# Attention with a forget gate and a SwiGLU block on one Trainium2 core: gate rows sent straight to their places, narrower crossbar turns, a clip on another engine, more fillers and a new order

## The chip, the cores and the metric

The kernel runs on one core of a Trainium2 chip. The core has five engines with instruction queues of their own: TensorE (PE in the profile; its weight loads are the row PEld), VectorE (DVE), ScalarE (ACT), GpSimd (POOL) and SyncE (SP, which here only issues DMAs). Each runs its own instructions in order and waits on semaphores for the others. TensorE writes to PSUM, which has eight banks of 128 x 512 fp32; ACT and DVE read from there. The metric is the device time of one execution in microseconds; each kernel has several runs, and their median counts.

## The reference

```python
scores = scale * np.matmul(q, k.transpose(0, 1, 3, 2))
log_f = np.log(np.clip(f, 0.0001, 1.0))
cum = np.cumsum(log_f, axis=-1)
decay = cum[:, :, :, None] - cum[:, :, None, :]
causal = np.triu(np.ones((S, S), dtype=bool), k=1)
scores = np.where(causal, -1000000000.0, scores + decay)
scores = scores - np.max(scores, axis=-1, keepdims=True)
attn = np.exp(scores)
attn = attn / (np.sum(attn, axis=-1, keepdims=True) + 1e-09)
return np.matmul(attn, v).astype(np.float32)
```

That is the attention, with 8 batches, 8 heads, 576 positions and 64 channels a head; scale is 1/8. Its output, laid out as x with 4608 tokens of 512 channels, goes through the feed-forward part with a width of 1536:

```python
g = x @ w_gate
silu = g * (1.0 / (1.0 + np.exp(-g)))
val = x @ w_val
return (silu * val @ w_out).astype(np.float32)
```

Inputs and output are fp32; inside, the kernel multiplies in bf16.

## The kernel before, in words

**Attention.** A head's scores are computed transposed, keys on the partitions. The causal half is cut into blocks of 128 keys by up to 320 queries, grouped into four PSUM banks (`BANKS`). For each bank PE computes the scores (`score`, L650; `score2`, L668 to L680, for batch 0), ACT takes the exponential into bf16 (`expo`, L684, tiles PTa for bank 0 and PT for the others), POOL zeroes the triangle above the diagonal (`mask`, L693), and PE multiplies the result with the values and a column of ones (`weigh`, L707). DVE divides by the sum (L714, L719), and PE transposes the head pair (`flip`, L724) and ACT or DVE copies it to xT (`put`), or a crossbar DMA does both (`cross`, L735).

**The decay.** The decay is added by the same matmul: beside the 64 channels, queries and keys have four more rows (partitions 64 to 67 of QK). On the query side they hold 8 times the cumulated logarithm and three rows of ones, on the key side one row of ones and the cumulated logarithm, times -8, in three bf16 parts. `gates` makes them: loads of f on SP and ACT, a clip (L334), the logarithm on ACT (L337), the scan on DVE (L341), then `hi`, `less`, `mid`, `less`, `low` (L346 to L357), in two column halves of 256 and 320 for the 16 heads of batches 0 and 1. Batch 0 reads its rows in place. For batch 1, `dec_out` writes four rows per head to a DRAM tensor, `blank` writes the ones there, and `rows` (L549) brings all of them to QK, a DMA per head pair. The other 48 heads (`lf1`, `cum1`) have a clip of their own on POOL, a logarithm on ACT, and their scan and parts later on. ACT loads the table of the Exp function (L478, `o_warm`) after all of these logarithms.

**Queries and keys.** Batch 0 and 1: POOL issues DMAs that convert to bf16 (`ld_quad`, L501), PE transposes (`turn_two`, L509, and `turn`, L525), and ACT or DVE copies from PSUM to QK, putting the columns in order (`straighten`, through L310 for ACT and L312 for DVE and POOL). Batches 2 to 7: a DMA on POOL's queue narrows a pair of heads to bf16 in DRAM (`narrow`), and two crossbar transposes on SP (`turned`, L546), one each for queries and keys, bring it to QK. A turn writes all 128 partitions, so `rows` follows it and overwrites partitions 64 to 67.

**The feed-forward part.** For each tile of 512 tokens: gate and value matmuls (L852; four accumulating matmuls are one group), the tanh on ACT (L856), two products on DVE (L860, L863), the projection (L867), a copy on ACT (L871), and the store on SP (L874). The first four chunks of the first tile are done in two halves of 256 tokens. Weights come by DMAs on POOL's queue (L845, L848).

**What sets the order.** Nothing is ordered by hand in the program text. Every step is an `Op` with the engines that can do it, an estimated duration, what it comes after, the buffers that it takes, a key and perhaps an earliest time. `Plan.run` walks through time, and whenever an engine is free it starts, of the steps that are ready and whose buffers are free, the one with the lowest key; that sequence becomes the engine's program order. A copy that ACT or DVE can do goes to whichever takes it first. The table `ORDER` replaces the key of a step by its number, counted in the order of creation. Where PE has nothing to start before 22 us of planned time (`IDLE_TO`), a filler matmul (`dummy`, L954) of 256 columns is put in, into a free bank of the pool f. Batches from 2 on are released at planned times, `PACE0` for the first of them.

Of the kernel before, what the change touches and what calls it, by code (L numbers as in the profile page):

```python
# [10 lines left out]
BF16 = mybir.dt.bfloat16  # L11
# [23 lines left out]
class Plan:  # L35
# [32 lines left out]
    def run(self, idle=None):  # L68
# [30 lines left out]
        while left:  # L99
# [45 lines left out]
            for e in engines:  # L145
                while busy[e] <= t + 1e-9:
# [61 lines left out]
PACE0 = 59.0  # L208
# [4 lines left out]
def kernel(ctx, tc, q, k, v, f, w_gate, w_val, w_out, out):  # L213
    nc = tc.nc
# [24 lines left out]
    qk_dram = nc.dram_tensor("qk_d", (2 * B, HSD + D), BF16, kind="Internal").ap()  # L239
# [116 lines left out]
    def low(e, c):  # L356
        nc.vector.tensor_scalar(out=KG[:, c], in0=r1[:, c], scalar1=ct[:, 2:3], scalar2=ct[:, 3:4], op0=ALU.mult, op1=ALU.add)  # L357
# [11 lines left out]
    def dec_out(e, b, n):  # L369
        g = slice(H, 2 * H) if b else slice(2 * H, BH)  # L370
        src = KG[2 * H * ((n - 1) % 4) + H :][:H] if b else late[n][2 * H :]
        nc.sync.dma_start(out=dec_dram[0, 0, g] if n == 0 else dec_dram[n, 1, g], in_=src)
# [13 lines left out]
    def gates(parts, key):  # L386
# [10 lines left out]
        for i, c in enumerate(parts):  # L397
# [3 lines left out]
            a = op(("DVE", 0.05 + w * 0.0011), hi, c, after=[s], key=kk, tag="hi")  # L401
            a = op(("DVE", 0.1 + w * 0.00155), less, 0, c, after=[a, o_ct], key=kk)
            a = op(("DVE", 0.05 + w * 0.0011), mid, c, after=[a], key=kk)
            a = op(("DVE", 0.1 + w * 0.00155), less, 1, c, after=[a], key=kk)
            a = op(("DVE", 0.05 + w * 0.0011), low, c, after=[a], key=kk, tag="low")
# [5 lines left out]
        outs = [op(("SP", SPi), dec_out, 1, n, after=ends, key=-7, dma=0.1, packet=50, tag="decout") for n in range(4)]  # L411
# [7 lines left out]
        out1 = [op(("SP", SPi), dec_out, 0, n, after=l, key=9000, ready=DECOUT_AT, dma=0.25, packet=50, tag="decout") for n in range(4)]  # L419
# [4 lines left out]
    def blank(e, what):  # L424
# [6 lines left out]
        elif what == "edge":  # L431
            nc.sync.dma_start(out=qk_dram[:, HSD:], in_=QK[: 2 * B, 0, 1, 2 * S :])
        elif what == "ones":
            E[e].memset(ones.bitcast(F32), ONE2)
        elif isinstance(what, tuple) and what[0] == "ones_q":
            nc.sync.dma_start(out=dec_dram[0, 1, what[1]], in_=ones[what[1]])
        elif isinstance(what, tuple):
            n = what[1].stop - what[1].start
            nc.sync.dma_start(out=dec_dram[1:, 0, what[1]].rearrange("r h s -> h r s"),
                              in_=ones[what[1]].unsqueeze(1).to_broadcast([n, 3, S]))  # L440
# [25 lines left out]
        else:  # L466
# [16 lines left out]
    o_edge = op(("SP", SPi), blank, "edge", after=[o_qkz], key=900, dma=0.2, ready=22)  # L483
    o_out1, o_out2 = [[op(("SP", SPi), blank, (x, c), after=[o_ones], key=1, dma=0.06 * n, packet=50, ready=t) for x in ("ones_q", "ones_k")]
                      for c, n, t in ((slice(0, 2 * H), 1, 4), (slice(2 * H, BH), 6, ONES_AT))]
# [56 lines left out]
    def turned(e, p, x):  # L542
        b, r = divmod(p, FB)
        lo = (2 * b + x) * (HSD + D) + 2 * r * S * D
        src = bass.AP(qk_dram.tensor, qk_dram.offset + lo, [[D, 2 * S], [1, P]])
        nc.sync.dma_start_transpose(out=QK[:, hqk[p].i, x, : 2 * S], in_=src)  # L546
# [23 lines left out]
    def values(b, n, key, ready=0.0):  # L570
# [9 lines left out]
        o = op(("SP", 0.9), ld_v, b, n, bv, after=held, behind=rows1 if b == 1 else out1 if b == 2 else [], take=[] if held else [bv], use=[bv] if held else [], key=key, dma=0.6 if last else 1.2, ready=ready, tag=("v", b, n))  # L580
# [10 lines left out]
    turns, rows1 = [], []  # L591
# [14 lines left out]
    def quad(b, g, key, ready=0.0):  # L606
# [12 lines left out]
        for u in range(2):  # L619
# [3 lines left out]
            for j in range(2):  # L623
                q_ready[2 * p + j] = done[u] + [r]
# [452 lines left out]
```

## Time and profile before

| | us |
|---|---|
| median of 3 runs | 383.69 (383.54 to 383.76) |
| the profiled execution | 383.79 |
| its span, first to last instruction | 382.0 |
| PE busy in the span | 373.3 |
| DVE, ACT, POOL busy | 217.6, 212.6, 142.9 |
| granted TensorE clock | 1.000 of full |

Each row of a stretch table gives the stretch, its length, then for each engine the busy time and in brackets the number of instructions. Rows of a timeline give start, duration, engine, line, operation, output and input tiles with their shapes, and in square brackets the idle time of the engine before it and what ended that. Adjacent instructions of one kind are merged to one row with their count. A matmul's duration includes its passage through the array, so that the durations of pipelined matmuls overlap. Rows of the chain of waits give start, time and work. Lines are those of the kernel before.

### The profile page before, as it was taken

The page shows a single profiled execution, that of the slowest core. Times are in us where ns is not written, and L with a number is a line of the kernel's source. Part 1 is how long each engine was busy: PE and PEld are TensorE (multiplying, and loading weights), DVE is VectorE, ACT ScalarE, POOL GpSimd, SP SyncE. Part 2 cuts the span into 40 slices and gives each one's busy share as a digit, 9 for nine tenths or more (in the row PEclk, how much of TensorE's full clock was granted, in tenths as well). Part 3 has the DMA queues.
Part 4 walks back from the last instruction along what each step waited for, and adds up shares of the span by engine and source line. Part 5 has one row for each costly group of instructions (what it writes and reads, how often), then busy time and mean ns, then how long its engine had stood idle before and what let it go on. Part 6 is the DMA issues. An engine that isn't in the chain of part 4 may idle for free.

```text
span 382.0 us, 8349 instructions
## 1 busy us (share of the span) xinstructions
PE 373.3 (98%) x3129; PEld 207.5 (54%) x3129; DVE 217.6 (57%) x454; ACT 212.6 (56%) x435; POOL 142.9 (37%) x369
## 2 busy tenths in 40 slices
PE   5999999999999999999999999999999999999996
PEld 4677665455555555555655555555654444444444
DVE  8887976277516771377326761576327815733750
ACT  4999872266466565844766466557763323323322
POOL 8996656035443453535463346513430000000000
PEclk9999999999999999999999999999999999999999
DMA  8999998759979975999799959993431011002003
GB/s 144 181 192 189 210 227 144 192 96 173 194 179 192 182 155 132 208 177 190 153 216 220 172 94 247 191 181 63 69 89 45 2 55 55 2 27 83 3 0 110
DMA packets 125000, 51.88 MB, mean 136 GB/s; under 512 B 111840, under 2 KB 119360, under 8 KB 124192
## 3 DMA queue, kind: packets, MB, share of 16 engines
q1 hardware_dynamic: 108608, 36.14, 47.2%
q0 software_dynamic: 16288, 15.14, 26.4%
q8 instruction: 24, 0.39, 0.4%
q14 instruction: 16, 0.13, 0.1%
q10 hardware_dynamic: 64, 0.07, 0.1%
HBM read 38.56 MB, written 17.07 MB: 146 GB/s over the span
## 4 chain that ended last, share of the span: by engine, by line
PE 93%; ACT 5%; issue 1%; DVE 1%; POOL 0%; ACTq 0%; POOLq 0%
PE ps L852 49%; PE ps L867 24%; PE ps L650 10%; PE ps L707 7%; ACT PT L684 1%; ACT QK L310 1%; PE ps L954 1%; ACT PTa L684 1%; PE ps L724 1%; ACT L478 0%; POOL xT L501 0%; PE ps L668 0%; ACT xT L310 0%; DVE xn L719 0%; PE ps L676 0%
## 5 line engine op out<-in xcount | busy, mean ns | idle before, releaser
L852 PE MATMUL ps<-xT,wv 128*128 128x512 bf16 (+1 forms) x448 | 111.5, 371 | 0.0
L856 ACT ACTIVATE th<-ps 128x512 f32<-128x512 f32 (+1 forms) x112 | 65.2, 583 | 83.0 <-PE ps L852 81.8
L852 PE MATMUL ps<-xT,wg 128*128 128x512 bf16 (+1 forms) x448 | 111.4, 371 | 0.0
L860 DVE SCALAR_TENSOR_TENSOR th<-th,ps 128x512 f32<-128x512 f32 (+1 forms) x112 | 74.5, 666 | 62.3 <-ACT th L856 61.9
L867 PE MATMUL ps<-wo,hh 128*128 128x512 bf16 (+2 forms) x456 | 104.9, 368 | 0.0
L684 ACT ACTIVATE PT<-ps 128x512 bf16<-128x512 f32 (+2 forms) x192 | 91.6, 513 | 15.5 <-PE ps L650 10.8
L863 DVE TENSOR_TENSOR hh<-th,ps 128x512 bf16<-128x512 f32 (+1 forms) x112 | 74.7, 668 | 13.0 <-PE ps L852 2.8
L693 POOL TENSOR_SCALAR_AFFINE_SELECT PT<-PT 128x128 bf16<-128x128 bf16 (+1 forms) x192 | 53.2, 283 | 54.1 <-ACT PT L684 48.7
L650 PE MATMUL ps<-QK 68*128 68x256 bf16 (+2 forms) x392 | 63.7, 260 | 0.8 <-ACT QK L310 0.6
L852 PEld LDWEIGHTS <-wg 128*128 128x128 bf16 x448 | 42.5, 97 | 40.4
L852 PEld LDWEIGHTS <-wv 128*128 128x128 bf16 x448 | 42.2, 97 | 39.7
L867 PEld LDWEIGHTS <-hh 128*128 128x128 bf16 x456 | 41.5, 97 | 36.3 <-issue 0.3
L693 POOL TENSOR_SCALAR_AFFINE_SELECT PTa<-PTa 128x256 bf16<-128x256 bf16 x64 | 26.1, 416 | 86.2 <-ACT PTa L684 84.7
L714 DVE RECIPROCAL rc<-ps 128x5 f32<-128x5 f32 (+2 forms) x68 | 12.9, 190 | 68.9 <-PE ps L707 68.2
L871 ACT ACTIVATE ot<-ps 128x512 f32<-128x512 f32 (+2 forms) x38 | 21.9, 575 | 52.2 <-PE ps L867 48.6
L707 PE MATMUL ps<-VB,PT 128*128 128x65 bf16 x768 | 43.7, 193 | 0.0
L707 PEld LDWEIGHTS <-PT 128*128 128x128 bf16 x768 | 35.7, 97 | 13.4 <-POOL PT L693 1.2
L650 PEld LDWEIGHTS <-QK 68*128 68x128 bf16 x392 | 31.9, 97 | 19.0 <-issue 1.4
L684 ACT ACTIVATE PTa<-ps 128x384 bf16<-128x384 f32 x64 | 30.9, 487 | 10.8 <-PE ps L650 10.8
L719 DVE TENSOR_TENSOR xn<-ps,rc 128x320 bf16<-128x320 f32 (+2 forms) x72 | 32.3, 454 | 2.3
L312 POOL CAST VB<-natv 128x512 bf16<-128x512 f32 (+1 forms) x32 | 19.0, 616 | 0.4 <-DMA natv<-in_v_dram 0.4
L707 PEld LDWEIGHTS <-PTa 128*128 128x128 bf16 x192 | 13.1, 97 | 10.9 <-POOL PTa L693 0.6
(71 smaller groups left out, 158.7 us busy)
## 6 DMA issues: line engine op xcount, KB each, us to landing
out_dram<-ot SPq DMA_DIRECT2D x35, 256.0 KB
natv<-in_v_dram SPq DMA_DIRECT2D x25, 256.0 KB
qk_d<-in_q_dram POOLq DMA_DIRECT2D x24, 144.0 KB, 3.6
qk_d<-in_k_dram POOLq DMA_DIRECT2D x24, 144.0 KB, 4.4
wv<-in_moe_w_val_dram POOLq DMA_DIRECT2D x3, 512.0 KB, 12.8
wg<-in_moe_w_gate_dram POOLq DMA_DIRECT2D x3, 512.0 KB, 10.1
wo<-in_moe_w_out_dram POOLq DMA_DIRECT2D x4, 384.0 KB, 15.6
xT<-in_q_dram POOLq DMA_DIRECT2D x4, 288.0 KB, 7.4
```

Source lines behind the costliest of these rows:

```text
L312: E[e].tensor_copy(dst, src)
L650: nc.tensor.matmul(s[:, c : c + w], QK[:KR, hqk[p].i, 1, j * S + kt * P : j * S + (kt + 1) * P], QK[:KR, hqk[p].i, 0, j * S + q0 : j * S + ...
L684: nc.scalar.activation(place(h, i)[:, OFFS[i] : OFFS[i] + c], ps(bs)[:, :c], AF.Exp, scale=0.125)
L693: nc.gpsimd.affine_select(out=d, in_=d, pattern=pat, compare_op=ALU.is_ge, fill=0.0, base=0, channel_multiplier=-1,)
L707: nc.tensor.matmul(o[:, lo : lo + D + 1], pt[:, c : c + P], VB[hvb[b].i][:, kt, hb, : D + 1], start=first and n == 0, stop=last and n == l ...
L719: nc.vector.tensor_mul(XN[bx.i][:, qb : qb + nq, j], o, r)
L852: nc.tensor.matmul(ps(bf)[:, :n], w[:, ko, fc * P : (fc + 1) * P], xT[:, ko, t0 : t0 + n], start=(ko == 0), stop=(ko == KD - 1))
L856: nc.scalar.activation(TH[bt.i][:, :n], ps(bf)[:, :n], AF.Tanh, scale=0.5)
L860: nc.vector.scalar_tensor_tensor(out=t, in0=t, scalar=1.0, in1=ps(bf)[:, :n], op0=ALU.add, op1=ALU.mult)
L863: nc.vector.tensor_mul(HH[bh.i][:, lo : lo + n], TH[bt.i][:, :n], ps(bf)[:, :n])
L867: nc.tensor.matmul(ps(bf)[:m, c], HH[hs[fc].i][:, lo : lo + m], wo[:, fc, c], start=(fc == 0), stop=(fc == KF - 1))
L871: nc.scalar.activation(OT[bo.i][:m, c], ps(bf)[:m, c], AF.Copy, scale=0.5)
```

## The change

1. Batch one's gate rows: eight copies `dec_in`, each of one row of four heads, go from the tile of the gates straight to QK, and four copies fill the rows of ones there. The two writes of ones to DRAM cover the other heads alone, and batch 1 has no `rows`.
2. `turned` reads 64 columns instead of 128 and writes partitions 0 to 63 alone. So `rows` touches nothing that a turn writes; it takes the slot and is issued ahead of the turns. The pad at the end of the DRAM tensor and the DMA that filled it go.
3. The clip of the 48 other heads is done by DVE instead of POOL.
4. `low` is a scalar_tensor_tensor whose second tensor is a broadcast column, instead of a tensor_scalar with two columns.
5. Fillers go to any free bank of the pools o, f and t, in that order, instead of f alone.
6. Some estimates of the planner (among them `TWARM`, the time from which it takes matmuls at full speed, and the cost of turns, straightens, `hi` and `mid`), `PACE0`, and the table `ORDER` are new. The exponentials of bank 0 of batch 0 name the Exp table's load as a predecessor. Steps of batch 0's second part and of the feed-forward part have a number higher by one than before.

```diff
-                        if e == "PE" and idle and idle[0].done is not None and idle[0].done <= t < idle[1] and self.free["f"]:
-                            idle[2](self.free["f"][-1])
+                        spare = [(p, self.free[p][-1]) for p in ("o", "f", "t") if self.free[p]]
+                        if e == "PE" and idle and idle[0].done is not None and idle[0].done <= t < idle[1] and spare:
+                            idle[2](spare[0])
...
-PACE0 = 59.0
+PACE0 = 58.0
...
     def low(e, c):
-        nc.vector.tensor_scalar(out=KG[:, c], in0=r1[:, c], scalar1=ct[:, 2:3], scalar2=ct[:, 3:4], op0=ALU.mult, op1=ALU.add)
+        nc.vector.scalar_tensor_tensor(out=KG[:, c], in0=r1[:, c], scalar=ct[:, 2:3], in1=ct[:, 3:4].to_broadcast([P, c.stop - c.start]),
+                                       op0=ALU.mult, op1=ALU.add)
...
-    def dec_out(e, b, n):
-        g = slice(H, 2 * H) if b else slice(2 * H, BH)
-        src = KG[2 * H * ((n - 1) % 4) + H :][:H] if b else late[n][2 * H :]
-        nc.sync.dma_start(out=dec_dram[0, 0, g] if n == 0 else dec_dram[n, 1, g], in_=src)
+    def dec_out(e, n):
+        g = slice(2 * H, BH)
+        nc.sync.dma_start(out=dec_dram[0, 0, g] if n == 0 else dec_dram[n, 1, g], in_=late[n][2 * H :])
+
+    def dec_in(e, n, j):
+
+        lo = 2 * H * ((n - 1) % 4) + H + j
+        dst = QK[D + n : D + n + 1, 2 : 2 + FB, min(n, 1), j * S : (j + 1) * S]
+        nc.sync.dma_start(out=dst, in_=KG[lo : lo + H - 1 : 2])
...
-        outs = [op(("SP", SPi), dec_out, 1, n, after=ends, key=-7, dma=0.1, packet=50, tag="decout") for n in range(4)]
+        outs = [op(("SP", SPi), dec_in, n, j, after=ends, key=-7 + 0.1 * j, dma=0.05, packet=50, tag="decin") for j in range(2) for n in range(4)]
...
+            w, j = what
+            r = slice(D, D + 1) if w else slice(D + 1, KR)
+            dst = QK[r, 2 : 2 + FB, w, j * S : (j + 1) * S]
+            nc.sync.dma_start(out=dst, in_=ones[: r.stop - r.start].unsqueeze(1).to_broadcast([r.stop - r.start, FB, S]))
...
-        lo = (2 * b + x) * (HSD + D) + 2 * r * S * D
-        src = bass.AP(qk_dram.tensor, qk_dram.offset + lo, [[D, 2 * S], [1, P]])
-        nc.sync.dma_start_transpose(out=QK[:, hqk[p].i, x, : 2 * S], in_=src)
+        lo = (2 * b + x) * HSD + 2 * r * S * D
+        src = bass.AP(qk_dram.tensor, qk_dram.offset + lo, [[D, 2 * S], [1, D]])
+        nc.sync.dma_start_transpose(out=QK[:D, hqk[p].i, x, : 2 * S], in_=src)
...
-            r = op(("SP", SPi), rows, p, after=[o_qkz] + out0 + o_out1, use=[hqk[p]], key=key, dma=0.25, ready=ready, tag=("rows", p))
-            rows1.append(r)
             for j in range(2):
-                q_ready[2 * p + j] = done[u] + [r]
+                q_ready[2 * p + j] = done[u] + out0[4 * j : 4 * j + 4] + o_out1[2 * j : 2 * j + 2]
...
-        ts = []
+        done = [op(("SP", SPi), rows, p, after=out1 + o_out2, take=[hqk[p]], use=[hqk[p]], key=key - 1, dma=0.25,
+                   ready=release(p) - ROWS_LEAD, tag=("rows", p))]
         for x in range(2):
-            ts.append(op(("SP", 1.45), turned, p, x, after=[narrowed[x], o_edge] + out1, behind=ts, take=[] if x else [hqk[p]],
-                         use=[hqk[p]] if x else [], key=key, dma=1.6, ready=release(p), tag=("turned", p)))
-        done = ts + [op(("SP", SPi), rows, p, after=ts + out0 + out1 + o_out2, use=[hqk[p]], key=key + 3, dma=0.25,
-                        tag=("rows", p))]
+            done.append(op(("SP", TURN_SP), turned, p, x, after=[narrowed[x]] + out1, behind=done, use=[hqk[p]] if x else [],
+                           key=key, dma=TURN_DMA, ready=release(p), tag=("turned", p)))
...
-TWARM = 8.3
+TWARM = 7.5
...
-CLIP1 = ("POOL", 2.2)
+CLIP1 = ("DVE", 0.75)
```

Of the new table, some entries, by step number. On DVE: `hi` of the first half 18 (-233.2), `less` 19 (-333.1), `mid` 20 (-73.1347), `less` 21 and `low` 22 (-115.6), the second scan 24 (197.6), the clip of the other heads 42 (-73.1347), the pad clears 59 (379.0), the ones 60 (59.8). Before, the pad clears had -78.4, the ones -14.0, and the clip -15.0. On ACT: the logarithm of the other heads 43 (-283.5) and the table's load 54 (-283.5), before -13 and -143.4. The straightens of the second pair of head pairs of batch 0, 80, 82, 84 and 86, have -87.8, -98.4, -13.7 and 59.8. On PE: the gate groups 1536 (1302.9) and 1516 (1570.7), before 100200 and 100000; the score groups 273 (1535.7) and 280 (1565.1) of batch 0's last heads; its last flips 289 and 293 (2012.1 and 1985.6).

More of the change, by code (lines that the diff above doesn't have):

```diff
@@ L418, in gates @@
             l.append(a)
-        out1 = [op(("SP", SPi), dec_out, 0, n, after=l, key=9000, ready=DECOUT_AT, dma=0.25, packet=50, tag="decout") for n in range(4)]
+        out1 = [op(("SP", SPi), dec_out, n, after=l, key=9000, ready=DECOUT_AT, dma=0.25, packet=50, tag="decout") for n in range(4)]
         return done, lns + [l1], outs, out1
@@ L589, in values @@
                 o.after.append(v_ready[b, 0])
-    turns, rows1 = [], []
+    turns = []
     def four(g, key):
```

36 lines of the change are left out of this document (17 added, 19 removed), and 92 rows, old and new, of the table ORDER.

## The prediction

> **What bounds the kernel now.** I began with the page's table of engines, and then took the busy time by stretch, cut where the chain of waits changes its character.
>
> ```profile
> PE 373.3 (98%) x3129; PEld 207.5 (54%) x3129; DVE 217.6 (57%) x454; ACT 212.6 (56%) x435; POOL 142.9 (37%) x369
> ```
> ```profile
> 0.00:7.20 7.20, 3.60 (x18) 2.32 (x20) 5.58 (x35) 2.79 (x5) 6.00 (x13) 1.00 0.74 125
> 7.20:16.00 8.80, 7.88 (x211) 5.88 (x213) 8.44 (x32) 8.11 (x16) 8.66 (x12) 1.00 1.56 177
> 16.00:24.00 8.00, 7.76 (x131) 5.21 (x127) 5.70 (x21) 8.00 (x22) 7.99 (x21) 1.00 1.39 202
> 24.00:31.65 7.65, 7.02 (x164) 5.59 (x159) 6.52 (x19) 7.28 (x16) 7.49 (x21) 1.00 1.55 186
> 31.65:60.00 28.35, 28.33 (x255) 18.56 (x253) 22.99 (x47) 23.50 (x53) 16.67 (x42) 1.00 1.18 204
> 60.00:368.50 308.50, 308.30 (x2293) 164.01 (x2292) 167.20 (x303) 160.16 (x321) 96.05 (x265) 1.00 0.67 128
> 368.50:382.00 13.50, 10.39 (x72) 5.92 (x70) 1.15 (x2) 2.73 (x6) 0.00 (x0) 1.00 0.22 78
> ```
>
> The columns are the length, then PE, PEld, DVE, ACT and POOL (busy us and instructions), the granted clock, the DMA share and GB/s. From 31.65, where the first gate matmul of the feed-forward part begins, to 368.5, PE is busy 336.63 of 336.85 us. Nothing that a DMA, VectorE or GpSimd does there can shorten the run unless PE gets less work, and the change removes no useful matmul. The last 13.5 us are the last projections and stores, which the diff leaves alone. So the change is decided in the first 31.65 us, and there ACT (23.39 of 24.45 us from 7.20 on) and POOL (24.14) are full, while PE stands still 24.45 - 22.66 = 1.79 us and fills part of the rest with filler matmuls. The chain of waits says which of the two full engines it is:
>
> ```profile
> 3.60 3.59 PE ps L954 x16
> 7.86 2.28 ACT QK L310 x4
> 10.14 0.54 ACT QK L337
> 10.70 1.28 ACT L478
> 13.46 0.53 ACT QK L310
> 17.80 2.89 ACT PT L684 x7
> 29.01 0.74 ACT QK L310
> 30.05 0.54 PE ps L650 x4
> 31.81 0.44 PE ps L852 x4
> ```
>
> Columns: start, length, work. Fillers (L954) hold PE until the first turned queries, then from 7.86 to about 20.7 (17.80 + 2.89) the chain is nearly ACT alone: straightens (L310), the logarithm of the other heads (L337), the load of the Exp table (L478), exponentials (L684). Later it alternates between PE, VectorE and ACT until the gates begin. The reader should see that a microsecond comes off the run only if ACT's chain shrinks or starts sooner, or if PE is given gate matmuls to do while it waits for ACT.
>
> **The change part by part.** The rows that price it:
>
> ```profile
> 7.54 2.14 POOL L334 TENSOR_SCALAR QK<-QK 64x576 f32<-64x576 f32 x1
> 3.74 1.42 DVE L334 TENSOR_SCALAR xT<-xT 64x256 f32<-64x256 f32 x4
> 6.96 0.48 DVE L350 SCALAR_TENSOR_TENSOR xT<-xT,ct 128x256 f32<-128x256 bf16 x1
> 7.48 0.88 DVE L357 TENSOR_SCALAR xT<-xT,ct 128x256 bf16<-128x256 f32 x1
> 11.01 0.65 DVE L430 MEMSET PT<- 128x32 f32 x15
> 11.58 0.71 DVE L312 COPY QK<-ps 128x576 bf16<-128x576 bf16 x1
> 12.30 0.30 DVE L434 MEMSET ot<- 64x288 f32 x1
> 13.67 0.62 DVE L350 SCALAR_TENSOR_TENSOR xT<-xT,ct 128x320 f32<-128x320 bf16 x1
> 14.32 0.92 DVE L357 TENSOR_SCALAR xT<-xT,ct 128x320 bf16<-128x320 f32 x1
> 15.27 1.66 SPq L372 DMA_DIRECT2D dec_d<-xT  x4
> 21.86 2.70 SPq L549 DMA_DIRECT2D QK<-dec_d  x4
> ```
> ```profile
> 7.86 1.74 ACT L310 ACTIVATE QK<-ps 128x576 bf16<-128x576 bf16 x3 [1.66 <-PE ps L509]
> 11.53 0.72 PE L954 MATMUL ps<-ident 128*128 128x256 bf16 x5
> L954 PE MATMUL ps<-ident 128*128 128x256 bf16 x20 | 3.2, 273 | 0.1
> PEld L707 <- POOL PTa L693: 0.6, 2, 0.4
> L546 SPq DMA_TRANSPOSE QK<-qk_d x48: 1183/1345/2402, 60.1 to 265.4; - x48
> ```
>
> *Clip of the other heads.* POOL loses 2.14 us between 7.54 and 9.75, where nothing else on it could run, so the weight and value loads queued behind it are issued up to 2.1 us sooner. PE waits for POOL's masks for 0.6 us (the row of PEld above), so on the path it is between -0.6 and 0; I take 0, since ACT is ahead of the masks in the chain. VectorE gains a clip of 576 columns. Its four clips, 1152 columns, took 1.42 us, hence 0.71. ACT's logarithm and table load wait for this clip, and both now have the lowest keys on ACT. ACT has one hole of 1.66 us, just before 7.86, that they could use. But the clip's key (-73.1347) equals that of `mid` and lies above those of the steps around it, so it runs behind the first half of the gate chain, which ends at 8.36 in this trace. Too late for the hole: 0, with -1.66 as the far end.
>
> *`low` with a broadcast addend.* The two TENSOR_SCALAR (0.88 and 0.92 us) become SCALAR_TENSOR_TENSOR, which on the same widths take 0.48 and 0.62: -0.40 and -0.30. With the clip VectorE stands at +0.01. If the broadcast addend runs no faster than today's form it is +0.71, in an engine busy 8.44 of 8.80 us. I take 0.
>
> *Keys on VectorE and ACT.* The pad clears (0.65) and the ones (0.30) go from keys of -78 and -14 to 379 and 60, behind the second half of the gate chain and the straightens (-88, -98, -14 for three of the four of the second pair of head pairs). That frees 0.95 us of VectorE while ACT has its straightens; each costs ACT 0.53 on the chain (row at 13.46) and VectorE 0.71 (row at 11.58). One or two move: -0.53 to -1.07, and I take -0.8, against 0 if none moves.
>
> *Batch one's gate rows.* Gone are four writes to DRAM (1.66 us of SP together), four reads from it (2.70), and two writes of ones; in their place stand eight short copies and four of ones. At the 0.42 us that one of L372 takes on SP (1.66 by 4), twelve are 5.0 us, against 4.36 us and two more issues that went. The rows arrive some microseconds sooner, as the reads began only at 21.86. Yet batch one's first score (30.05) follows a straighten in the chain: 0. Batch one's last value loads on SP, which queued behind the reads, now queue behind the eight copies, no later than now.
>
> *Crossbar turns of 64 columns, rows ahead of them.* 48 turns, 1.345 us of SP each, the first at 60.1, in the stretch where PE stands still 0.20 us in 308.5. If they halve, -0.6 us of SP apiece, or stay, nothing follows: 0. The row copy moves ahead of two turns on the same queue; it waits for the slot's last score, as the first turn did, and the turns queue behind it, 0.7 us later at worst (2.70 by 4). What hides it is that no score waits for its turns in that stretch; that cover gone, a score waits 0.7. The edge copy goes, 0.
>
> *More fillers.* One costs (0.72 - 0.27) / 4 = 0.11 us of PE. There are 20 in the stretch after 7.20; 1.79 us of standstill holds at most 16 more, which cost nothing if they fall where PE waits anyhow, and up to 16 x 0.11 = 1.8 if each falls ahead of work that is ready. I take 0, as ACT and not PE leads there.
>
> *The order searched anew.* Before, gate groups have keys from 2000 up, behind every score of batch 0 (1801 at most). After, group 1536 (chunk 2 of the first tile's first half) has 1302.9 and 1516 has 1570.7, ahead of the last flips of batch 0 (1985.6 and 2012.1) and the former ahead of a score of its last heads (273, at 1535.7). A group of four matmuls is 0.44 us (row at 31.81); one of them in the holes takes 0.44 off what is left for later, and 1.79 us of holes bound it. I take -0.5.
>
> Sum: -0.8 - 0.5 = -1.3 us. The profiled execution took 383.79 us, 1.79 beyond its span, and the median of the runs is 383.69; 383.69 - 1.3 = **382.4**.
>
> The Trainium skill, "SBUF — State Buffer", section "SBUF: two separate sides", says that GpSimd cannot write the descriptors of its DMAs while VectorE runs an operation in a two-port mode, which by the section "Who interferes with whom" a tensor_scalar may enter. That speaks against putting the clip on VectorE. Here four such clips ran from 3.74 to 5.16 beside these issues:
>
> ```profile
> 4.29 0.71 POOL L501 DMA_DIRECT2D xT<-in_q_dram  x1
> L501 POOL DMA_DIRECT2D xT<-in_q_dram x4: 714/730/896, 1.3 to 15.7; - x4
> ```
>
> The issue at 4.29 took 0.71, the least of its kind, so the trace shows no such block. By the rule POOL would get back at most 0.71 of its 2.14 us and the sum would stay, as no POOL time is counted in it.
>
> **The rivals.** *Nothing moves.* ACT's work from 7.86 on is the same sum, and an order that permutes it without lightening it ends at the same time; the gates then begin at 31.65 as now. For it: ACT is full from 16 to 24, and VectorE has hardly more room than before. Against it: VectorE is only 5.70 of 8.00 busy from 16 to 24. Time 383.7.
>
> *Slower: a gate group moved ahead waits for its weights.* PE runs in order, so the scores behind such a group stand still, and ACT with them. The loads' landing:
>
> ```profile
> L848 POOL DMA_DIRECT2D wv<-in_moe_w_val_dram x3: 760/772/814, 9.8 to 27.1; - x3
> DMA to landing us min/median/max: 6.4/11.4/15.9
> ```
>
> From the median to the longest is 4.5 us. If the first group stands three microseconds before its weights, with the gain of 1.3 kept otherwise, the time is 385.4; from 1.3 us late on it is slower than now, and from 2.1 on measurably. The three are my choice, two thirds of that spread. For it: the spread. Against it: POOL can issue these loads 2.1 us sooner.
>
> *Fillers in front of ready work.* 16 of them, +1.8, the gain of 1.3 kept: 384.2; without the gain 385.5. It decides from 12 fillers on the path.
>
> *The narrower turn is not done by the crossbar.* The Trainium skill, "DMA: Bandwidth & Descriptors", section "DMA Transpose (X-bar)", says that for inputs with fewer than 128 columns software can fall back to rearranged accesses with inefficient descriptors; the page of the profile has no turn of that width. As a mechanism here: a turn would be 1152 x 64 = 73,728 pieces. The hardware queue's rate is this:
>
> ```profile
> q1 hardware_dynamic: 108608, 36.14, 47.2%
> ```
>
> 47.2% of 16 engines for 382 us is 2885 us of engine time, 27 ns a packet; 73,728 pieces are 2.0 ms over 16 engines, 122 us a turn and 5.9 ms for 48. So the run would take some 6 ms.
>
> **How the numbers follow.** Two tenths of a per cent, 0.77 us, is what a measurement here can tell from no change: faster ends at 382.92, slower begins at 384.46. The forecast has 0.50, its own range 380.8 (full -1.07 and -1.79) to 382.9. Nothing moves: 0.23, same. Late weights: 0.16, slower, 384.5 to 386. Fillers: 0.09, of which 0.07 slower and 0.02 same. The fallback: 0.02, slower. That makes faster 0.50, same 0.25, slower 0.25. The range from 380.8 to 385.5 leaves out the fallback, the dearer third of late weights and some 0.08 of the forecast beyond its bounds.
>
> **What would show it.** Right: the first gate matmul begins near 29 to 31, ACT's straightens from 7.2 to 16 drop from the seven of the row below to five or six, POOL shows no L334, PE's standstill before the gates falls below 1.3 us, and after 32 nothing changes. `low` at 0.5 to 0.6 and the clip near 0.7 confirm VectorE's balance. Wrong: PE idle in front of L852 released by a DMA (late weights), a row of L954 next to late scores (fillers), PE idle after 60 released by QK (turns), or the gates beginning at 31.65 as now.
>
> ```profile
> 7.20:16.00 8.80, 4.16 (x7) 1.00 1.56 177
> ```
>
> This row is of L310 on ACT alone: the length, ACT's busy time and instructions.

## The result and the profile after

The changed kernel takes 4735.85 us (median of 6 runs, 4723.47 to 4751.5) against 383.62 us before (6 runs too): 12.34 times as long, with an interval of 12.31 to 12.37. The forecast was 382.4 us in a range from 380.8 to 385.5. The profiled execution took 4740.25 us, with a span of 4738.5. Here and below, ratios leave out runs that took over 1.5% more than the fastest of their kernel, while medians and spreads are of all runs unless the text says otherwise.

From the page of the changed kernel, its table of engines, two rows of the slices, the hardware queue of the DMAs, the costliest group, and the issues of the turns:

```profile
PE 425.5 (9%) x3095; PEld 228.1 (5%) x3143; DVE 218.2 (5%) x460; ACT 214.2 (5%) x430; POOL 140.2 (3%) x368
...
PEclk8555555555555555555555555555555555555559
DMA  9999999999999999999999999999999999999991
...
q1 hardware_dynamic: 3591358, 28.95, 178.9%
...
L656 PE MATMUL ps<-QK 68*128 68x256 bf16 (+3 forms) x392 | 80.5, 314 | 4302.8 <-DMA QK<-qk_d 4302.7
...
QK<-qk_d SPq DMA_DIRECT2D x48, 144.0 KB
```

VectorE, ACT and POOL have about the work of before, and PE 425.5 us instead of 373.3, at a granted clock that is half for most of the span; PE stands still for some 4300 us, and nearly all of it stands in one row: the scores (L656, the old L650) wait for queries and keys. The last row says why. The 48 turns were DMA_TRANSPOSE before and are now DMA_DIRECT2D, an ordinary copy. The queue's packets grew from 108,608 to 3,591,358, that is by 3.48 million, while its bytes fell from 36.14 to 28.95 MB. 48 turns of 1152 x 64 elements are 3.54 million elements: one packet per two-byte element, less the 48 x 1152 = 55,296 packets of whole rows that the wide turns had. The granted clock is half in all the slices in which PE waits.

The stretch table of the changed kernel, with the columns of the one quoted in the prediction:

```profile
7.20:31.65 24.45, 24.34 (x503) 17.73 (x496) 22.00 (x74) 23.46 (x51) 22.36 (x50) 1.00 1.49 191
31.65:60.00 28.35, 28.17 (x254) 18.40 (x256) 23.32 (x50) 21.75 (x47) 14.68 (x38) 1.00 1.20 197
60.00:368.50 308.50, 19.80 (x184) 11.40 (x186) 8.51 (x21) 7.94 (x16) 7.54 (x20) 0.54 1.85 6
368.50:4700.00 4331.50, 314.27 (x1956) 160.87 (x1995) 142.19 (x258) 147.18 (x292) 89.60 (x249) 0.53 1.84 7
```

Up to 60 us nothing is wrong. Then PE is busy 19.80 of 308.5 us, and the DMAs move 6 GB/s at a share of 1.85. (A share above 1 means that the packets' times overlap: the share counts the time of every packet, not an engine's occupation.) SP's own queue and the waits, in the same kernel (start, length, work; then the time waited, how often, and the longest):

```profile
56.01 0.66 SPq L555 DMA_DIRECT2D QK<-qk_d  x1
63.43 91.11 SPq L880 DMA_DIRECT2D out_dram<-ot  x1
154.59 0.61 SPq L555 DMA_DIRECT2D QK<-qk_d  x1
155.25 92.19 SPq L880 DMA_DIRECT2D out_dram<-ot  x1
```
```profile
PE ps L656 <- DMA QK<-qk_d: 4302.7, 24, 187.5
```

The issue of a narrow turn (L555) takes SP only 0.66 us, but the next DMA on SP, a store of an output tile (L880), is held for 91.11 us. There are 24 waits, one per head pair of batches 2 to 7, and the longest, 187.5 us, is two turns of 93.8 us.

### The profile page after: what moved, and what is told of

Its sections match the earlier page's. It is cut to its first block, busy times and chain, and to the rows that moved or that the text cites. A ratio compares the mean times of both kernels' runs of the same rounds, so it can differ in the third digit from the quotient of the medians.

```text
span 4738.5 us, 8360 instructions
## 1 busy us (share of the span) xinstructions
PE 425.5 (9%) x3095; PEld 228.1 (5%) x3143; DVE 218.2 (5%) x460; ACT 214.2 (5%) x430; POOL 140.2 (3%) x368
## 3 DMA queue, kind: packets, MB, share of 16 engines
q1 hardware_dynamic: 3591358, 28.95, 178.9%
## 4 chain that ended last, share of the span: by engine, by line
another core or an unknown queue 91%; PE 8%; POOL 0%; issue 0%; DMA 0%; ACT 0%; ACTq 0%; POOLq 0%
PE ps L858 4%; PE ps L873 2%; PE ps L656 1%; PE ps L713 1%; DMA VB<-in_v_dram 0%; POOL VB L564 0%; POOL PT L699 0%; POOL xT L510 0%; POOL PTa L699 0%; PE ps L730 0%; ACT PT L690 0%; PE ps L534 0%; POOL wg L854 0%; POOL wv L854 0%
## 5 line engine op out<-in xcount | busy, mean ns | idle before, releaser
L656 PE MATMUL ps<-QK 68*128 68x256 bf16 (+3 forms) x392 | 80.5, 314 | 4302.8 <-DMA QK<-qk_d 4302.7
L656 PEld LDWEIGHTS <-QK 68*128 68x128 bf16 x392 | 36.6, 114 | 4334.2 <-DMA QK<-qk_d 2710.2
L858 PE MATMUL ps<-xT,wg 128*128 128x512 bf16 (+1 forms) x435 | 122.0, 404 | 1.4 <-issue 0.9
L858 PE MATMUL ps<-xT,wv 128*128 128x512 bf16 (+1 forms) x430 | 121.9, 405 | 1.0 <-issue 0.2
L713 PE MATMUL ps<-VB,PTa 128*128 128x65 bf16 x192 | 17.3, 206 | 0.0
```

The source lines that it names most:

```text
L656: nc.tensor.matmul(s[:, c : c + w], QK[:KR, hqk[p].i, 1, j * S + kt * P : j * S + (kt + 1) * P], QK[:KR, hqk[p].i, 0, j * S + q0 : j * S + ...
L713: nc.tensor.matmul(o[:, lo : lo + D + 1], pt[:, c : c + P], VB[hvb[b].i][:, kt, hb, : D + 1], start=first and n == 0, stop=last and n == l ...
L858: nc.tensor.matmul(ps(bf)[:, :n], w[:, ko, fc * P : (fc + 1) * P], xT[:, ko, t0 : t0 + n], start=(ko == 0), stop=(ko == KD - 1))
```

## Experiments

The theory from the two traces is that a turn of fewer than 128 columns is not done by the crossbar but in two-byte pieces, and that this accounts for the whole slowdown. Rivals are that the rest of the change (the rows ahead of the turns, the new order) has a part in it, that the price is a fixed one per turn, and that only very narrow turns are affected. A second question is what the other parts are worth once the turn is out of the way, since the forecast had 1.3 us for them.

**The turn as before, the rest as changed.**

```diff
-        src = bass.AP(qk_dram.tensor, qk_dram.offset + lo, [[D, 2 * S], [1, D]])
-        nc.sync.dma_start_transpose(out=QK[:D, hqk[p].i, x, : 2 * S], in_=src)
+        src = bass.AP(qk_dram.tensor, qk_dram.offset + lo, [[D, 2 * S], [1, P]])
+        nc.sync.dma_start_transpose(out=QK[:, hqk[p].i, x, : 2 * S], in_=src)
```

The pad in DRAM and its fill come back, and so does the row copy's place behind the turns, because a wide turn overwrites its four partitions. (Rows ahead of wide turns were therefore not tried.)

> The changed kernel with the turns of 128 columns as before (the pad at the end of the DRAM tensor, and the row copy behind the turns); all the rest of the change stays. Theory A, the turn of 64 columns has left the crossbar and this alone costs the 4350 us: the run falls to the sum of the other parts, 382.4 us, between 380.8 and 383.7; the packets on SP's queue are back near 110,000 and PE does not wait for QK. Theory B, the new place of the row copy or the new order starves PE as well: still well above 384.5 us, with PE waiting for QK or for weights after 32 us.

Measured: 389.35 us, ratio to before 1.0073, 95% interval [1.0035, 1.0111]. The 4.35 ms are gone, so they belonged to the turn, or to the place of the row copy, which went back with it; the next run tells the two apart. But the rest is slower than before, not 1.3 us faster, and its 12 runs spread from 384.26 to 395.27 (the median of the 7 that the ratio uses is 387.34). In its profiled execution (385.71 us) PE waited for the row copy behind the turns:

```profile
PE ps L660 <- DMA QK<-dec_d: 1.7, 2, 1.5
```

**The narrow turn alone, in the kernel before.**

```diff
-        src = bass.AP(qk_dram.tensor, qk_dram.offset + lo, [[D, 2 * S], [1, P]])
-        nc.sync.dma_start_transpose(out=QK[:, hqk[p].i, x, : 2 * S], in_=src)
+        src = bass.AP(qk_dram.tensor, qk_dram.offset + lo, [[D, 2 * S], [1, D]])
+        nc.sync.dma_start_transpose(out=QK[:D, hqk[p].i, x, : 2 * S], in_=src)
```

> The kernel before, with the turns of 64 columns alone (source and destination of the turn; order, rows, clip and fillers as before). Theory A: about 4700 us, 3.5 million packets more on SP's queue, each pair of heads held for about 187 us as in the changed kernel. Theory B, the narrow turn is harmless and another part starves PE: 384 us or less.

Measured: 4764.44 us (one run). Its hardware queue, from the page, and the first row of its waits:

```profile
q1 hardware_dynamic: 3591488, 29.06, 180.3%
```
```profile
PE ps L650 <- DMA QK<-dec_d: 3254.8, 17, 361.2
```

The narrow turn is enough by itself. The releaser is the row copy here because in this kernel it follows the turns on SP; it is late because the turns are. The waits are fewer and longer than the 187 us for each pair that I expected. Further rows of PE's waits, 1065 us in sum, name POOL, ACT and another DMA as the releaser, and were not followed back.

**One narrow turn of the 48,** the queries of pair 31 in the kernel before.

```diff
+        if (p, x) == (31, 0):
+            src = bass.AP(qk_dram.tensor, qk_dram.offset + lo, [[D, 2 * S], [1, D]])
+            nc.sync.dma_start_transpose(out=QK[:D, hqk[p].i, x, : 2 * S], in_=src)
+        else:
+            nc.sync.dma_start_transpose(out=QK[:, hqk[p].i, x, : 2 * S], in_=src)
```

> The kernel before with one single turn of 64 columns, that of the queries of the last pair of heads (31); the other 47 are as before. Theory A, a narrow turn has a price of its own, the engine time of 73,728 packets: 74,000 packets more, PE waits for QK once, and as half of the changed kernel's longest wait (187 us for two turns) is 94 us, of which the feed-forward tiles of earlier tokens cover some 20 to 35 us, the run is 440 to 460 us. Rival, the price comes from many narrow turns standing in one another's way: a single one is nearly hidden, below 400 us.

Measured: 471.72 us. SP's queue, PE's longest wait, the packets from 300 to 340 us, and the stretch from 285 to 290 us:

```profile
264.56 0.71 SPq L548 DMA_DIRECT2D QK<-qk_d  x1
265.33 93.46 SPq L550 DMA_TRANSPOSE QK<-qk_d  x1
```
```profile
PE ps L654 <- DMA QK<-dec_d: 86.2, 2, 85.7
```
```profile
q1 hardware_dynamic: 31890, 0.06, 194.9%
```
```profile
285.00:290.00 5.00, 0.00 (x0) 0.00 (x0) 0.00 (x0) 0.00 (x0) 0.00 (x0) 0.50 1.95 2
```

One narrow turn holds the next DMA on SP for 93.46 us and costs the run 88 us (471.72 - 383.79 = 87.93). That is more than the 440 to 460 us that I expected: PE's longest wait is 85.7 us, so that other work covered 8 us of the hold and not 20 to 35. In 40 us 31,890 packets moved 0.06 MB, two bytes each; over 16 engines that is 40 x 16 / 31,890 = 20.1 ns a piece, and 73,728 pieces are 92.5 us. With PE at 0.00 busy, the granted clock fell to 0.50: it falls while PE stands still, and does not cause the wait, which ends with the DMAs that are held.

**Half of the rows narrow,** to tell a price per piece from a price per turn.

```diff
+        if (p, x) == (31, 0):
+            for j, w in ((0, D), (1, P)):
+                src = bass.AP(qk_dram.tensor, qk_dram.offset + lo + j * S * D, [[D, S], [1, w]])
+                nc.sync.dma_start_transpose(out=QK[:w, hqk[p].i, x, j * S : (j + 1) * S], in_=src)
```

> The kernel before, with the queries of pair 31 turned head by head: the first head's 576 rows with 64 columns, the other's with 128. By the theory that a narrow turn is moved in pieces of two bytes at a fixed price each, half the pieces (36,864) take half the 85.7 to 93.5 us that the one whole narrow turn of the earlier run cost: PE stands still about 43 to 47 us for QK, and the profiled execution is near 428 us against 471.72. The rival is a fixed price for each narrow turn, whatever its size (a switch of the queue's mode, or a wait for it to run empty): then PE stands still about 85 us again and the execution stays near 470 us.

**112 columns,** to find where the crossbar ends.

```diff
+        w = 112 if (p, x) == (31, 0) else P
+        src = bass.AP(qk_dram.tensor, qk_dram.offset + lo, [[D, 2 * S], [1, w]])
+        nc.sync.dma_start_transpose(out=QK[:w, hqk[p].i, x, : 2 * S], in_=src)
```

> The kernel before, with the queries of pair 31 turned with 112 columns. By the theory that any turn of fewer than 128 columns leaves the crossbar, 1152 x 112 = 129,024 pieces are moved, 1.75 times those of 64 columns: PE stands still 150 to 165 us for QK, and the profiled execution is 535 to 550 us. The rival is that only a turn of 64 columns or fewer leaves it, and that one of 112 (seven times 16) is still done by the crossbar: then PE waits for no QK, and the execution is 383 to 386 us.

Measured: 429.12 us with half of the rows, 537.5 us with 112 columns, near the 428 and within the 535 to 550 of the theory. SP's queue and PE's wait, first with half of the rows:

```profile
266.84 47.90 SPq L549 DMA_TRANSPOSE QK<-qk_d  x1
```
```profile
PE ps L655 <- DMA QK<-dec_d: 41.8, 2, 41.4
```

And with 112 columns:

```profile
264.64 160.34 SPq L548 DMA_TRANSPOSE QK<-qk_d  x1
```
```profile
PE ps L652 <- DMA QK<-dec_d: 151.6, 1, 151.6
```

The hold on SP is 47.90, 93.46 and 160.34 us for 36,864, 73,728 and 129,024 pieces: 20.8, 20.3 and 19.9 ns a piece and engine. The price is one per piece, not per turn. A turn of 112 columns leaves the crossbar too, and below 128 a turn takes longer the *more* columns it has, while at 128 it takes SP 1.345 us (the row of L546 in the prediction). Widths from 113 to 127 were not run.

**The turns planned at the cost of before.** The first run had kept the planner's new estimates of a turn, 1.4 us on SP and 1.0 for the DMA, which suit no turn that was run.

```diff
-            ts.append(op(("SP", TURN_SP), turned, p, x, after=[narrowed[x]] + out1, behind=ts, take=[] if x else [hqk[p]],
-                         use=[hqk[p]] if x else [], key=key, dma=TURN_DMA, ready=release(p), tag=("turned", p)))
+            ts.append(op(("SP", 1.45), turned, p, x, after=[narrowed[x]] + out1, behind=ts, take=[] if x else [hqk[p]],
+                         use=[hqk[p]] if x else [], key=key, dma=1.6, ready=release(p), tag=("turned", p)))
```

> As e1_wide_turns, but the planner costs a turn as before (1.45 us of SP and 1.6 of the DMA engines instead of 1.4 and 1.0), so that the order from batch 2 on is made for turns of 128 columns. If the 5 us of e1_wide_turns came from turns that arrive later than its plan says: PE's waits for QK after 60 us (1.7 us in its profile) go and the time is 383 to 384, with little spread from run to run. If the new order of the first 60 us is at fault: it stays near 389.

Measured: 385.78 us (385.14 to 389.01), ratio 1.0058 [1.0033, 1.0083]. PE's wait for the row copy is gone from its profile, but it still is slower than the kernel before. Two rows of its stretch table:

```profile
7.20:31.65 24.45, 24.31 (x500) 17.78 (x501) 21.42 (x73) 23.02 (x50) 22.35 (x50) 1.00 1.48 190
...
150.00:160.00 10.00, 9.56 (x92) 5.53 (x91) 2.24 (x7) 7.08 (x17) 5.00 (x15) 1.00 1.08 200
```

Ahead of the gates PE's standstill fell from 1.79 us to 0.14, as I had wanted. What PE does instead is seen in the same stretch of the filler's line alone (length, PE, PEld, clock, DMA share, GB/s), first before, then in this run:

```profile
7.20:31.65 24.45, 3.23 (x20) 1.56 (x20) 1.00 1.50 188
```
```profile
7.20:31.65 24.45, 4.82 (x34) 3.00 (x34) 1.00 1.48 190
```

The standstill lost 1.65 us and the fillers gained 1.59. Without the fillers PE's work in the stretch is 19.43 us before and 19.49 here. The holes were not closed but filled; the work that is ready did not come sooner. Over the whole span the sum is: standstill 8.7 us before (382.0 - 373.3) and 7.8 here (383.6 - 375.8), so -0.9; fillers 6.8 and 8.4 us in all, +1.6; PE's other work +0.9. Together +1.6, the difference of the spans. That other work is no more matmuls and no slower ones: the two groups that grew, L717 (the old L707) with PT from 43.7 to 45.0 us and the projections from 104.9 to 105.6, have the same counts and mean durations (193 and 368 ns), so that they overlap less among themselves. Why they do is not shown.

**Without the additional fillers,** those that the rule of before would not have placed being planned but not emitted: once on the run with the new estimates of a turn, once on the one with those of before.

```diff
         z = bank[bank_of[i[0]] + i[1]]
+        if not plan.free["f"]:
+            return
```

> As e1_wide_turns, but a filler that the rule of before would not have given (no free bank in pool f) is left out; the order of everything else is the same. Fillers cost nothing, as the prediction took it: equal to e1_wide_turns within 0.2 us. Rival of the prediction, fillers in front of ready work: up to 1.5 us faster than e1_wide_turns (14 fillers at 0.11 us). Third, the fillers keep TensorE's clock up: slower than e1_wide_turns, with matmuls before 30 us spaced wider.

> As e5_wide_planned, without the fillers that the rule of before would not have given; the order of everything else is the same. The prediction took the fillers at 0: equal to e5_wide_planned within 0.3 us. The profiles of e1_wide_turns and e4_fewer_fillers differ by about 2 us of PE work done by 36 us, to the credit of the fillers: if that is theirs, 1 to 3 us slower than e5_wide_planned.

Measured: 389.62 us, ratio 1.0081 [1.0046, 1.0116], and 387.06 us, 1.0078 [1.0059, 1.0097]. Both intervals overlap with those of the runs with fillers, and neither run is faster: of the runs that the ratios use, the medians are 387.30 against 387.34 us in the first pair and 387.06 against 385.78 in the second. In the stretch from 7.20 to 31.65, 27 of the 34 fillers are gone. So the rival "fillers in front of ready work" finds no support, though a small cost of theirs could be hidden by another loss. The filler's line in the two runs:

```profile
7.20:31.65 24.45, 2.05 (x7) 0.83 (x7) 1.00 1.48 190
```
```profile
7.20:31.65 24.45, 1.41 (x7) 0.64 (x7) 0.93 1.48 191
```

Both have 7 fillers in this stretch. In the second the granted clock is 0.93, and at 0.93, 24.45 us of PE's time are worth an estimated 1.7 us less, near the 1.3 us between the last two medians. But in the first it is 1.00, as it is with 20 or 34 fillers. Over the whole span the clock lay at 0.996 or lower in 6 of 6 runs of the second kernel, against 1 of 9 with its fillers, and in 9 of 12 of the first, against 5 of 12. So fewer fillers go with a lowered clock more often, but not always, and that they cause it is not shown.

**Parts alone, in the kernel before with its program order kept.** First the clip of the other heads on VectorE and `low` with a broadcast addend:

```diff
-        E[e].tensor_scalar(out=lf[:, c], in0=src[:, c], scalar1=1e-4, scalar2=1.0, op0=ALU.max, op1=ALU.min)
+        (nc.vector if lf is lf1 else E[e]).tensor_scalar(out=lf[:, c], in0=src[:, c], scalar1=1e-4, scalar2=1.0, op0=ALU.max, op1=ALU.min)
...
-        nc.vector.tensor_scalar(out=KG[:, c], in0=r1[:, c], scalar1=ct[:, 2:3], scalar2=ct[:, 3:4], op0=ALU.mult, op1=ALU.add)
+        nc.vector.scalar_tensor_tensor(out=KG[:, c], in0=r1[:, c], scalar=ct[:, 2:3], in1=ct[:, 3:4].to_broadcast([P, c.stop - c.start]),
+                                       op0=ALU.mult, op1=ALU.add)
```

> The kernel before with its order kept, and two steps issued otherwise: the clip of the other heads on DVE at its old place in time, and low as scalar_tensor_tensor with a broadcast addend. The prediction has the clip at 0.71 us, low at 0.48 and 0.62, VectorE at +0.01, POOL at -2.14: within 0.3 us of before, or up to 1.7 faster if the clip fills ACT's hole ahead of 7.86. If the clip stands in front of the gate chain and that counts, 0.4 to 0.7 slower.

Then batch one's gate rows and ones, sent by twelve direct copies, in place of its four row copies:

```diff
+        if b:
+            for j in range(2):
+                lo = 2 * H * ((n - 1) % 4) + H + j
+                dst = QK[D + n : D + n + 1, 2 : 2 + FB, min(n, 1), j * S : (j + 1) * S]
+                nc.sync.dma_start(out=dst, in_=KG[lo : lo + H - 1 : 2])
+            return
...
+        if p < 2 * FB:
+            return
```

> The kernel before with its order kept, and batch one's gate rows and ones sent straight to QK by twelve short copies; its four row copies are not issued. The prediction has this at 0, as batch one's first score followed a straighten: within 0.2 us of before. Rival: the rows were late too (they began at 21.86), and PE's 0.6 us of waiting at 30 goes: 0.3 to 0.6 faster.

And both diffs together:

> The kernel before with its order kept, and three parts of the change that stay in place: the clip of the other heads on VectorE, low with a broadcast addend, and batch one's gate rows and ones by twelve direct copies. The two earlier runs gave 0.9994 (clip and low) and 0.9992 (direct rows), both with 1 in their intervals. If the two gains are real and add up, the ratio is about 0.9986, some 383.1 us, and this is the fastest version so far. If they are nothing, as my sum had it for each of them (0), it is 0.999 to 1.001. If what made the change with wide turns slower (1.0058 to 1.0078) were in these parts and not in the order, the fillers and the planner's estimates, it would be 1.005 or more.

Measured: 383.47 us, 0.9994 [0.9978, 1.0010], for clip and `low`; 383.38 us, 0.9992 [0.9976, 1.0008], for the direct rows; 382.72 us, 0.9973 [0.9955, 0.9992], for both. The last is faster than both kernels: the median is 1.15 us below that of its own comparison (383.87), and the interval of the ratio amounts to 0.3 to 1.7 us. The sum of the two single gains, 0.9986, lies in that interval, so the runs do not show that the parts do more together than apart. The stretch table of both together:

```profile
7.20:31.65 24.45, 23.29 (x504) 16.90 (x505) 21.18 (x73) 23.79 (x53) 22.41 (x51) 1.00 1.51 193
31.65:60.00 28.35, 28.33 (x252) 18.29 (x250) 22.82 (x48) 23.46 (x52) 16.66 (x43) 1.00 1.12 195
60.00:150.00 90.00, 90.00 (x752) 50.11 (x751) 48.70 (x95) 47.67 (x98) 36.36 (x98) 1.00 0.88 165
150.00:160.00 10.00, 10.00 (x101) 6.11 (x100) 2.52 (x6) 7.74 (x17) 5.01 (x15) 1.00 1.01 164
160.00:368.50 208.50, 208.50 (x1446) 108.04 (x1445) 116.71 (x203) 104.39 (x206) 53.84 (x152) 1.00 0.58 111
```

It has the 20 fillers of before in the first of these stretches, and PE stands still there 1.16 us instead of 1.79; after 60 us PE is without a gap where before it lacked 0.20. These 0.83 us are most of the 1.1 by which the span is shorter (380.9 against 382.0). With no more fillers, less standstill is a gain here. The profiles of the single parts divide it: in the first of these stretches PE stands still 1.03 us with clip and `low` and 1.50 with the direct rows, and its wait of 0.6 us for a straighten is gone in the former and 0.3 in the latter. After 60 us PE has no gap with the direct rows, but lacks 1.19 us with clip and `low`, most of it in one wait for a row copy:

```profile
PE ps L651 <- DMA QK<-dec_d: 1.0, 1, 1.0
```

Each of these is one execution, that of clip and `low` (384.32 us) above the median of its kernel, so how often such a wait comes is not shown.

**The changed kernel with wide turns and the old keys.** Each key of the old table stands at the step that has its place now; the new estimates stay.

```diff
-PACE0 = 58.0
+PACE0 = 59.0
...
-    0: -73.1337, 1: -8.5751, 2: -69.6672, 3: -73.1327, 4: -73.1357, 5: -73.1367, 6: -1212.1615, 7: -74.3612, 8: -1212.1605, 9: -8.5731,
+    0: 107.3799, 1: -115.0092, 2: -89.8956, 3: -29.9951, 4: 101.5875, 5: -25.999, 6: 65.2884, 7: -115.0072, 8: 16.5943, 9: -115.0082,
...
```

> The changed kernel with turns of 128 columns, planned at the cost of before, and with the keys and the release time of before (each old number put at the step that now has its place); the new estimates, the wider choice of banks for fillers and the other parts stay. With the new keys this was 385.78 us (1.0058); the three parts in the order of before gave 382.72 us (0.9973). If the new keys are what lost those 3.1 us, this is 382.3 to 383.5 us. If the new estimates, which shift what the planner puts first, or the fillers lost them, it stays at 385 us or above. Where my prediction's term for the new order (a gain of 0.5 us, and 0.8 us for the keys on VectorE) were right and only something else hid it, this would be slower than the run with the new keys: 386.5 to 387.5 us.

Measured: 390.02 us, ratio 1.0168 [1.0128, 1.0208], slower by 4.2 us than with the new keys and beyond what I expected in any case. The loss begins early, in the stretch from 16 to 24 us, where ACT, full before (8.00 of 8.00) and at 7.59 with the new keys, has a hole:

```profile
16.00:24.00 8.00, 6.97 (x100) 4.83 (x100) 6.53 (x26) 4.83 (x12) 6.30 (x12) 1.00 1.36 203
```

Fillers stand in the holes here too: 52 in the stretch from 7.20 to 31.65, where the new keys have 34, and PE's work without them is 15.41 us there against 19.49. So the new keys are better than the old ones under the new estimates, but keys, estimates and fillers together (385.78) are 3.1 us slower than the three parts in the old order (382.72). Which of them loses the 3.1 us stays open: keys and estimates set the order together, and old estimates with the new keys were not run.

## Why the prediction was wrong, point by point

**The step that failed** is "Crossbar turns of 64 columns, rows ahead of them", priced at 0 because "If they halve, -0.6 us of SP apiece, or stay, nothing follows: 0." The new turn was in no row of the trace of before, and I bounded it by two ends that both suppose a crossbar. The runs show a third case: 73,728 pieces of two bytes and 93 us a turn. The narrow turn alone gives 4764 us, and with wide turns the rest is at 386 to 389. The cover that the prediction relied on, "no score waits for its turns in that stretch", cannot hide a hold of 93 us: the sign named for being wrong here, PE idle after 60 released by QK, came with 4302.7 us.

**The rival "the narrower turn is not done by the crossbar"** is what happened, with a chance of 0.02. Its mechanism was right and its price a third too high: 122 us a turn against 93. The term that was mis-sized is the time of a packet, 27 ns from a queue whose packets have 333 bytes on average (36.14 MB by 108,608), against 20 ns measured for pieces of two bytes. That the price came so near has some luck in it. The 27 ns were a packet's own time, read from the queue's share, and by the same reading a two-byte packet takes longer, not shorter: 194.9% of 16 engines for 40 us by 31,890 packets is 39 ns. But a share of 1.95 means that on average about two are under way on an engine at a time, which the prediction's row, at 47.2%, could not show. 48 x 90.6 us are the 4350 us between the changed kernel and the run with wide turns planned as before (4735.85 - 385.78).

The Trainium skill, "DMA: Bandwidth & Descriptors", section "DMA Transpose (X-bar)", says that for a DRAM input with a free dimension under 128 software *can* fall back to a rearranged access pattern. The runs with 64 and with 112 columns agree, and here it did so each time. The Trainium skill, "DMA: Bandwidth & Descriptors", section "Rules for kernel authors", puts a plain DMA with a rearranged access pattern at a 19-fold difference to the hardware transpose. By that, a turn would have been an estimated 26 us (19 times 1.345). Here SP is held 93.46 us against 1.345, 69-fold, and the measurement decides. I did not use that sentence in the prediction. The chance of 0.02 set a stated rule, with no row against it, below rivals of a microsecond.

**New order (-0.5) and keys on VectorE (-0.8).** Most signs named for them came. In the changed kernel, ACT's straightens from 7.20 to 16 (L311 alone: length, ACT's time and instructions), VectorE's `low` and its clip, and PE's first gate group:

```profile
7.20:16.00 8.80, 3.47 (x6) 1.00 1.64 188
```
```profile
7.74 0.48 DVE L358 SCALAR_TENSOR_TENSOR xT<-xT,ct 128x256 bf16<-128x256 f32 x1
8.14 0.52 DVE L335 TENSOR_SCALAR QK<-QK 64x576 f32<-64x576 f32 x1
...
11.54 0.55 DVE L358 SCALAR_TENSOR_TENSOR xT<-xT,ct 128x320 bf16<-128x320 f32 x1
```
```profile
27.66 0.61 PE L858 MATMUL ps<-xT,wg 128*128 128x256 bf16 x4
```

Six straightens instead of seven, the first gate at 27.66 instead of 31.65 (29 to 31 was named), PE's standstill at 24.45 - 24.34 = 0.11 us, and no clip on POOL. Not so "after 32 nothing changes", even with wide turns: planned at the cost of before, PE lacks 0.51 us from 60 to 368.5 where it lacked 0.20. And yet with wide turns the kernel is 1.0058 to 1.0073 of before. The sign "standstill below 1.3" was badly chosen: fillers satisfy it as well as useful work does, and 34 of them instead of 20 took the place of the holes. The gain of 1.3 us is not borne out; the sum over the span is +1.6.

**Fillers (0).** There are 14 more in the stretch, within the 16 allowed, and with 27 fewer the run is not faster: nothing speaks for the rival "fillers in front of ready work". **Late weights** fall: in no profile with wide turns does PE wait for weights. **"Nothing moves"** would have been nearest for the other parts, yet they are slower, by 0.3 to 1.1%, and which step of the sum for them failed is known only so far: useful work did not come sooner, and PE's work and standstill after 60 us grew.

**Clip, `low`, direct rows (0 each).** Each alone is within 0.2% of no change, as the sum had it. The clip did not fill ACT's hole, and `low` took 0.48 and 0.55 us where I had taken 0.48 and 0.62. The clip took 0.52 to 0.61 where I had 0.71. Together they gave 1.15 us (0.3 to 1.7), where the sum had nothing. I had allowed the clip up to 0.6 us through PE's wait for POOL's masks and taken 0. That wait, 0.6 us in a row of PEld, is 0.2 in the profiles of both runs with the clip on VectorE and 0.6 with the direct rows alone, so part of this term may be the gain. For the direct rows I had taken 0 because batch one's first score follows a straighten; that wait halved with them.

## What to carry to other kernels

When a change gives an instruction a shape that the trace does not show, the rows of the old shape bound nothing: look whether the same operation is still issued (DMA_TRANSPOSE or DMA_DIRECT2D, packets against bytes), and time one such instruction in a working kernel before 48 are changed. A crossbar turn like these, which needs only 64 columns, is better left at 128, with the surplus overwritten, than made narrow. And count idle time together with fillers: a bubble that is filled is not a bubble that is gone.

## What the hardware did that I had not expected

- A turn in two-byte pieces costs 20 ns a piece and engine, counted over 16 engines, whatever their number (36,864 to 129,024). The DMA behind it on SP was held until it was nearly done, a turn (93.46 us) as well as a store (91.11).
- While PE stood still for long, the granted clock was 0.50. In a stretch with 7 fillers instead of 20 it was 0.93 in one profile and 1.00 in another.
- VectorE's `hi` of the first half took 0.29 us before and 0.57 in the run with clip and direct rows, `mid` 0.29 and 0.66, each beside issues of GpSimd's DMAs. In the changed kernel `hi`, beside such issues, took 0.29 again. The first two rows are of the run with clip and direct rows, the last is of the changed kernel:

```profile
6.01 0.57 DVE L346 TENSOR_SCALAR xT<-xT 128x256 bf16<-128x256 f32 x1
...
7.55 0.66 DVE L354 TENSOR_SCALAR xT<-xT 128x256 bf16<-128x256 f32 x1
```
```profile
6.04 0.29 DVE L347 TENSOR_SCALAR xT<-xT 128x256 bf16<-128x256 f32 x1
```

The Trainium skill, "SBUF — State Buffer", section "Who interferes with whom", has the one of VectorE and GpSimd that comes second blocked, if VectorE's operation runs in a two-port mode. The two long rows can be such blocks; by the short one not every such meeting blocks, and no run tells apart when it does.
